# Own weights beside the turned rows in one bank, their turn behind the output products, values products with 128 columns

## The chip, the cores and the metric

The kernel runs on one core of a Trainium2 chip. The metric is the device time of one execution in microseconds (us). A core has TensorE (PE; its weight loads are shown apart as PEld), VectorE (DVE), ScalarE (ACT), GpSimd (POOL) and SyncE (SP, which issues DMAs). Products land in PSUM, which has eight banks; VectorE and ScalarE copy from there. TensorE's clock has two granted levels, 1.2 and 2.4 GHz, shown as 0.50 and 1.00.

## What is computed

An attention layer with a decaying state, and behind it two mixture-of-experts layers over the same 3072 tokens. The change lies in the attention:

```python
for t in range(S):                                   # B=4, H=8, S=768, D=48
    kt, vt, rt, wt = (k[:, :, t], v[:, :, t], r[:, :, t], w[:, :, t])
    cur = np.einsum('bhd,bhe->bhde', u[None] * kt, vt)
    y[:, :, t] = np.einsum('bhd,bhde->bhe', rt, state + cur)
    state = wt[:, :, :, None] * state + np.einsum('bhd,bhe->bhde', kt, vt)
...
x = y as 3072 rows of 384                            # then:
x = moe(x, one expert of 8 by argmax of x @ w_gate)
return moe2(x, two experts of 8, with noise)
```

## The kernel before

The sequence is cut into chunks of C = 128 tokens, which makes NU = 24 units (six chunks of four batch rows). A unit holds all eight heads, as four pairs (HP = 4, `pr`), the two heads of a pair at partitions 0 and 64 of the turned inputs. The unit's output is a sum of three parts: products of the tokens of the same chunk (scores, masked, times values), products with the state carried in from the chunk before, and each token's own product, which is weighted by `r u k` summed over the head ("own weights").

One loop (line 850) runs over i = 0 to 24 as a software pipeline: it works on units i + 2, i, i - 1 and i - 2 at once. The schedule is written out by hand: each engine runs its instructions in the order in which the loop body issues them, and waits where an operand or a bank is not ready. SP issues the loads (three of 224 KB and one of 192 KB per unit) and the store of the unit's 128 output rows; POOL masks the scores and scatters table entries.

In TensorE's order a loop has:

- `scores(i)` (L645), eight products into the banks `sp0` and `sp1`; ScalarE copies them to `at`, POOL masks `at`.
- `kv(i-1)`: eight products of keys and values (L670) into the first columns of bank `pp`, then four products of `ub` and `q` (L673), which give the own weights per head pair, into columns 256 to 383 of the same bank. ScalarE copies those to `oT` (L676).
- `keys(i)`: four transposes (L658) into bank `kp`, copied by ScalarE to `kk` (L660).
- `xt(i-2)`: three transposes (L742) of the output rows `x` of unit i - 2 into bank `xp`, copied by ScalarE to `xT` (L744) for the gates.
- `own(i-1)`: one product that turns `oT`, so that tokens lie on partitions (L682), into columns 400 to 407 of bank `pp`.
- `yout(i-1)`: from the second chunk on eight products with the carried state (L713), then eight of the masked scores and the values (L720), into the double bank `b45`. A head needs 48 columns; the products read 96 (the values of the next head come along and are not used), the last head 48.
- `logits(i-2)`: products with the gates (L192) in column groups, and for the last unit of a group their turn (L197).

A product of 32-bit floats is two instructions in the trace. In VectorE's order a loop has the carried state (`carry_on`, L701), the first scan of unit i + 2 (L615), the output rows `x` of unit i - 2 (`rows_out`, L732, which reads bank `b45` and `sv`), the rest of `prep(i+2)` (L618 to L630), in twelve loops a split of expert weights on VectorE or POOL (L165), then `s` (`kv_add(i-1)`, L697, which reads bank `pp`) and `sv` (`bonus(i-1)`, L688, which reads the turned own weights). Units form groups of four, later of two. Three loops behind a group's last unit VectorE chooses the experts (`choose`, L202 to L264), woven into the list above; a loop later it places the tokens (`place`, L282 to L302). The ranks between them are products into bank `kp` (`rank`, L273). In the first four units ScalarE forms `s`.

`filler` (L771) issues products of 512 columns that nobody reads, in the first two loops and ahead of them. Behind the loop `early` begins the first expert's products (L177 to L179) in the same banks.

Of the kernel before, what the change touches and what calls it, by code (L numbers as in the profile page):

```python
# [9 lines left out]
F32 = mybir.dt.float32  # L10
# [9 lines left out]
B, H, S, D = 4, 8, 768, 48  # L20
N, DM, E, F = B * S, H * D, 8, 1024
C = 128
NC = S // C
NU = NC * B
HP = H // 2
PP = 112
KD = DM // 128
# [39 lines left out]
def rwkv_moe_kernel(ctx, tc, r, k, v, w, rT, kT, wT, rkv, u, g1, a1, a2, g2, noise, b1, b2, out):  # L67
    nc = tc.nc
# [9 lines left out]
    ident = con.tile([128, 128], F32, name="ident")  # L78
# [43 lines left out]
    def banks(pool, **plan):  # L122

        turns = {n: itertools.cycle(b) for n, b in plan.items()}
        return lambda name: pool.tile([128, 512], F32, name="b" + next(turns[name]))
# [370 lines left out]
    with ExitStack() as c2:  # L496
        pa = c2.enter_context(tc.tile_pool(name="pa", bufs=1, space=PSUM))
        ac = c2.enter_context(tc.tile_pool(name="ac", bufs=1))
        wk = c2.enter_context(tc.tile_pool(name="wk", bufs=2))
# [3 lines left out]
        T = {}  # L503
        NS = HP * (C + 1)
        bank = banks(pa, sp0="0", sp1="1", kp="2", pp="3", xp="6", lp="7")

        def bank2():

            return pa.tile([128, 2, 512], F32, name="b45")
# [4 lines left out]
        def quads(t, n=128):  # L514
            return t[:, 0:HP * n].rearrange("p (a b) -> p a b", a=HP)
# [3 lines left out]
        for i in range(3):  # L519
            t = ac.tile([PP, NS + 1], F32, name=f"decay{i}")  # L520
# [23 lines left out]
        start = []  # L544
        for i in range(2):
            t = ac.tile([PP, HP, C + 1], F32, name=f"start{i}")
# [4 lines left out]
        ub = ac.tile([PP, HP, 32], F32, name="ub")  # L551
# [38 lines left out]
        def fills(i):  # L590
            if i == 1:
                nc.vector.memset(z, 0.0)
                nc.vector.memset(empty, 0)
                nc.vector.memset(empty[:, :, 0], N)
            if i in (2, 3):
                clear_table((tab1, tab2)[i - 2])
            if i == 4:
                nc.sync.dma_start(xrow[0:N, DM:XW], noise)
            if i == 5:
                nc.sync.dma_start(xrow[N:N + 1, 0:DM], z[0:1, :])  # L600
            if i == 6:
                nc.sync.dma_start(xrow[N:N + 1, DM:XW], z[0:1, 0:E])
            if i == 8:
                u0 = EARLY + 3
                b, n = u0 % B, NU - u0
                nc.sync.dma_start(rows(xrow, (b * S + (NC - 1) * C) * XW, [[XW, C], [S * XW, n], [1, DM]]),
                                  z[:, None, :].to_broadcast([C, n, DM]))
# [52 lines left out]
                nc.scalar.copy(t["kk"], kp[:, :, 0:PP])  # L660

        def kv(i):

            t = T[i]
            p = bank("pp")
            if i < NU - B:
                pp = t["pp"] = quads(p[:PP], D)
                for pr in range(HP):
                    for r0, r1, c0 in ((0, 64, 0), (64, PP, D)):
                        nc.tensor.matmul(pp[r0:r1, pr, :], t["kk"][:, pr, r0:r1],  # L670
                                         t["v"][:, pr * 96 + c0:pr * 96 + c0 + D], start=True, stop=True)
            for pr in range(HP):
                nc.tensor.matmul(p[32 * pr:32 * pr + 32, 256:256 + C], ub[:, pr, :], t["q"][:, pr, :],  # L673
                                 start=True, stop=True)
            t["oT"] = wk.tile([128, C], F32, name="oT", bufs=1)
            nc.scalar.copy(t["oT"], p[:, 256:256 + C])  # L676
            t["own"] = p[:C, 400:400 + H]

        def own(i):

            t = T[i]
            nc.tensor.matmul(t["own"], t["oT"], ident.rearrange("p (a b) -> p a b", a=HP)[:, :, 0:2],  # L682
                             start=True, stop=True)

# [5 lines left out]
        def kv_add(i):  # L690
            t = T[i]
            if i < NU - B:
                t["s0"] = wk.tile([PP, HP, D], F32, name="s0", bufs=4)
                if i < B:
                    nc.scalar.copy(t["s0"], t["pp"])
                else:
                    nc.vector.tensor_tensor(t["s0"], t["pp"], carry[i % B], OP.add)  # L697
# [5 lines left out]
        def yout(i):  # L703

            t = T[i]
            c, b = divmod(i, B)
            y = bank2()
            y = y.rearrange("p h (a d) -> p h a d", a=HP)
            if c:
                for pr in range(HP):  # L710
                    for hh in range(2):
                        r0 = 64 * hh
                        nc.tensor.matmul(y[:, hh, pr, 0:2 * D], t["R"][r0:r0 + D, pr, :],  # L713
                                         wide[b][r0:r0 + D, pr:pr + 2, :].rearrange("p a d -> p (a d)"),
                                         start=(pr == 0), stop=False, skip_group_check=True)
            for pr in range(HP):
                for hh in range(2):
                    h = 2 * pr + hh
                    n = min(2, H - h) * D
                    nc.tensor.matmul(y[:, hh, pr, 0:n], t["at"][:, hh, pr, :], t["v"][:, h * D:h * D + n],  # L720
                                     start=(c == 0 and pr == 0), stop=True, skip_group_check=True)
            t["y"] = y[:, :, :, 0:D]
# [12 lines left out]
            for g in T.get("eg", ()):  # L735
                tc.declare_no_dep(st.ins, g.ins, reason=APART)

        def xt(i):
            t = T[i]
            xp = quads(bank("xp"))[:, 0:KD]  # L740
            for k in range(KD):
                nc.tensor.transpose(xp[:, k, :], t["x"][:, k * 128:(k + 1) * 128], ident)  # L742
            t["xT"] = wk.tile([128, KD, C], F32, name="xT")
            nc.scalar.copy(t["xT"], xp)  # L744

        LAST, RT = {}, {}
        for u0, n in GROUPS:
# [102 lines left out]
        for i in range(NU + 1):  # L850
            on = [0 <= i - j < NU for j in range(4)]
            if i == 2:
                late_consts()
            fills(i)
            if i + 4 < NU:
                load(i + 4)
            if i + 3 < NU:
                load_rows(i + 3)
            rt = RT.get(i - 3)
            early_rt = rt if i == EARLY + 3 else None  # L860
            choose = rt.choose() if rt else none
            place = RT[i - 4].place() if i - 4 in RT and i != EARLY + 4 else none
            pre = prep(i + 2) if i + 2 < NU else none
            take(choose)
            if on[3]:
                carry_on(i - 3)
            take(choose)
            take(pre)
            if on[2]:
                rows_out(i - 2)  # L870
            for _ in range(3):
                take(choose)
                take(place, 3)
                take(pre)
            take(choose, 9)
            take(place, 9)
            take(pre, 9)
            if 8 <= i < 20:
                w_split(0, 0, *divmod(i - 8, 3), nc.gpsimd if i % 3 else nc.vector)
            if i in KICKS:  # L880
                kick()
            if on[0]:
                scores(i)
            if i == EARLY + EG:
                early_gather()
            if on[1]:
                kv(i - 1)
            if on[0]:
                keys(i)
            if on[2]:  # L890
                xt(i - 2)
            if rt:
                rt.exps()
            if on[1]:
                kv_add(i - 1)
                own(i - 1)
                yout(i - 1)
                bonus(i - 1)
            if on[2]:
                logits(i - 2)  # L900
            if rt:
                rt.rank(bank("kp"))
            if on[2]:
                turn(i - 2)
            if i - 4 in RT and i != EARLY + 4:
                waiting += [(RT[i - 4], j) for j in range(RT[i - 4].nj)]
            if early_rt:
                take(rt.place(), 9)
                waiting += [(rt, j) for j in range(rt.nj)]
            n = 2 if i < EARLY + 3 else len(waiting)  # L910
            for q, j in waiting[:n]:
                q.enter(j, "tab1")
            waiting = waiting[n:]
            if early_rt:
                early_load()
            if i < 2:
                filler(FB[i])
            if 5 <= i < 17 and (i - 5) % 3 == 0:
                w_load(0, 0, (i - 5) // 3)
            if i + 2 < NU:  # L920
                guard(i + 2)
# [5 lines left out]
        p = bank("kp")  # L927
# [166 lines left out]
    with ExitStack() as c2:  # L1094
        wk = c2.enter_context(tc.tile_pool(name="m1", bufs=2))
        bank = banks(psum, hp="01", tp="23", yp0="4", yp1="5", yp2="6", lp="7", up="01456")
# [185 lines left out]
    with ExitStack() as c2:  # L1282
        wk = c2.enter_context(tc.tile_pool(name="m2", bufs=1))
        bank = banks(psum, hp0="01", tp="23", hp1="45", yp="76")
# [163 lines left out]
```

## Time and profile before

| | us |
|---|---|
| median of 3 runs | 1031.95 |
| lowest and highest of them | 1031.88, 1053.61 |
| the profiled execution | 1035.67 |
| its span, first to last instruction | 1034.0 |

Over the span TensorE is busy for 970.8 us (94%), VectorE for 513.2, ScalarE for 396.5 and POOL for 404.8. The busy share mixes stages: the attention loop lies in the first 272 us, the expert layers behind it. A record of a matmul runs from its start to its modelled end, and pipelined records overlap, so the pace of a row of products is read from the distance of their starts.

### The profile page before, as it was taken

To read this page: it belongs to the slowest core of one execution; us is meant where nothing else is said; L and a number is where in the kernel's file an instruction comes from. 1 tells how busy PE (TensorE), PEld (TensorE's weight loads), DVE (VectorE), ACT (ScalarE), POOL (GpSimd) and SP (SyncE) were. 2 spreads that over 40 slices of the span, in tenths; PEclk is the share of its full clock that TensorE was granted. 3 is DMA by queue.
4 is the path that set the end of the run, shared out by engine and by line. 5 is a ranking of instruction groups with operands and counts; after the bars stand their busy time and mean duration, and the time that the engine had idled before them with its cause. 6 is when DMAs were issued, how large, how long until landed. Compare 5 with 4: busy or idle time off the path is not lost. (4 is left out here: it accounts for less than half of the span.)

```text
span 1034.0 us, 16583 instructions
## 1 busy us (share of the span) xinstructions
PE 970.8 (94%) x6212; PEld 867.7 (84%) x6212; DVE 513.2 (50%) x1162; ACT 396.5 (38%) x869; POOL 404.8 (39%) x562
## 2 busy tenths in 40 slices
PE   7789788988988999999999989999999999999996
PEld 4678677877778888999998778898989898989996
DVE  7955656465233456555666425715354453625220
ACT  4523433332213445455554315424343343434321
POOL 4214334223213165865885544233241514132303
PEclk8955665555559899999999989999999999999998
DMA  9717344330105555767564145453544434444303
GB/s 207 208 57 180 86 114 122 78 86 16 38 20 152 163 113 154 168 184 191 153 138 146 23 107 135 138 100 90 122 95 93 106 95 87 121 78 138 39 6 42
DMA packets 91100, 113.40 MB, mean 110 GB/s; under 512 B 26002, under 2 KB 68895, under 8 KB 91000
## 3 DMA queue, kind: packets, MB, share of 16 engines
q1 hardware_dynamic: 65848, 80.87, 28.1%
q0 software_dynamic: 25152, 31.27, 16.6%
q8 instruction: 54, 0.88, 0.4%
q14 instruction: 46, 0.38, 0.2%
HBM read 86.96 MB, written 25.78 MB: 109 GB/s over the span
## 5 line engine op out<-in xcount | busy, mean ns | idle before, releaser
L108 POOL DMA_INDIRECT out<-yo,ent x54 | 84.5, 1566 | 276.8 <-ACT yo L1339 224.5
L177 PE MATMUL b<-xhi,w1h 128*128 128x512 f32 (+8 forms) x384 | 133.1, 347 | 0.0
L179 PE MATMUL b<-xhi,w1l 128*128 128x512 f32 (+8 forms) x384 | 132.2, 344 | 0.0
L178 PE MATMUL b<-xlo,w1h 128*128 128x512 f32 (+8 forms) x384 | 132.2, 344 | 0.0
L1083 DVE TENSOR_TENSOR xlo<-b,xhi 128x512 fp32r<-128x512 f32 (+8 forms) x48 | 27.1, 570 | 157.2 <-ACT xhi L1082 157.2
L650 POOL TENSOR_SCALAR_AFFINE_SELECT at<-at 128x512 f32<-128x512 f32 x48 | 45.0, 958 | 132.2 <-ACT at L649 132.2
L1339 ACT ACTIVATE yo<-b,ent 128x384 f32<-128x384 f32 (+1 forms) x48 | 27.9, 581 | 167.6 <-issue 128.2
L1326 PE MATMUL b<-w2h,hah 128*128 128x384 f32 x256 | 89.2, 348 | 0.4 <-PEq L1274 0.4
L1328 PE MATMUL b<-w2h,hal 128*128 128x384 f32 x256 | 87.3, 341 | 0.0
L1327 PE MATMUL b<-w2l,hah 128*128 128x384 f32 x256 | 87.2, 341 | 0.0
L108 POOL DMA_INDIRECT tab<-en,si x60 | 77.8, 1296 | 19.1 <-issue 14.0
L177 PEld LDWEIGHTS b<-xhi,w1h 128*128 128x128 f32 x384 | 72.3, 188 | 11.8 <-issue 3.1
L178 PEld LDWEIGHTS b<-xlo,w1h 128*128 128x128 f32 x384 | 72.4, 189 | 8.8 <-DVE xlo L1083 0.2
L179 PEld LDWEIGHTS b<-xhi,w1l 128*128 128x128 f32 x384 | 72.3, 188 | 8.6
L177 PE MATMUL b<-hh,w2h 128*128 128x224 f32 (+7 forms) x216 | 75.4, 349 | 3.4 <-PEq L950 3.4
L177 PE MATMUL b<-xh,w1h 128*128 128x224 f32 (+7 forms) x216 | 77.2, 358 | 0.2 <-ACT xh L1129 0.2
L720 PE MATMUL b<-v,at 128*128 128x96 f32 (+1 forms) x384 | 77.3, 385 | 0.0
L720 PEld LDWEIGHTS b<-v,at 128*128 128x128 f32 x384 | 73.7, 295 | 3.2 <-issue 2.7
L178 PE MATMUL b<-xl,w1h 128*128 128x224 f32 (+7 forms) x216 | 74.3, 344 | 0.1
L179 PE MATMUL b<-xh,w1l 128*128 128x224 f32 (+7 forms) x216 | 74.2, 343 | 0.0
L178 PE MATMUL b<-hl,w2h 128*128 128x224 f32 (+7 forms) x216 | 73.2, 339 | 0.0
L179 PE MATMUL b<-hh,w2l 128*128 128x224 f32 (+7 forms) x216 | 73.1, 339 | 0.0
(221 smaller groups left out, 2246.4 us busy)
## 6 DMA issues: line engine op xcount, KB each, us to landing
raw<-in_a SPq DMA_DIRECT2D x32, 768.0 KB, 6.0
raw<-in_b SPq DMA_DIRECT2D x30, 768.0 KB, 5.0
decay<-in_wT SPq DMA_DIRECT2D x24, 224.0 KB, 4.5
kT<-in_kT SPq DMA_DIRECT2D x24, 224.0 KB, 4.4
rT<-in_rT SPq DMA_DIRECT2D x24, 224.0 KB, 4.3
v<-in_rkv SPq DMA_DIRECT2D x24, 192.0 KB, 4.4
xrow<-x SPq DMA_DIRECT2D x24, 192.0 KB, 4.3
out<-z SPq DMA_DIRECT2D x6, 768.0 KB, 10.1
```

Of the source, the lines that this page charges most:

```text
L108: st = nc.gpsimd.indirect_dma_start(out=table, out_offset=bass.IndirectOffsetOnAxis(ap=idx, axis=0), in_=src, in_offset=None, bounds_check ...
L177: nc.tensor.matmul(ps, st[0], mv[0], start=start, stop=False)
L178: nc.tensor.matmul(ps, st[0], mv[1], start=False, stop=False)
L179: nc.tensor.matmul(ps, st[1], mv[0], start=False, stop=stop)
L650: nc.gpsimd.affine_select(at[:, hh], at[:, hh], [[0, HP], [1, C]], OP.is_gt, 0.0, base=0, channel_multiplier=-1)
L720: nc.tensor.matmul(y[:, hh, pr, 0:n], t["at"][:, hh, pr, :], t["v"][:, h * D:h * D + n], start=(c == 0 and pr == 0), stop=True, skip_group ...
L1083: nc.vector.tensor_tensor(t["lo"][:, k], p[:, 0:n], t["hi"][:, k].bitcast(F32), OP.subtract)
L1326: nc.tensor.matmul(parts[0], h[:, f, sl], wh, start=(f == 0), stop=False)
L1327: nc.tensor.matmul(parts[0], h[:, f, sl], wl, start=False, stop=False)
L1328: nc.tensor.matmul(parts[0], l[:, f, sl], wh, start=False, stop=(f == NF - 1))
L1339: nc.scalar.activation(o, y, AF.Copy, scale=wgt2[:q, e, j:j + 1])
```

## The change

Four edits, which go together:

- The four products of `ub` and `q` (L673) leave bank `pp` and `kv`. They stand behind the transposes of `xt`, in the free fourth quarter of bank `xp`, and one ScalarE copy of up to 512 columns takes both to a tile of KD + 1 parts.
- `own` runs behind `yout`, and writes its eight columns to bank `kp`.
- The ranks of a group go to bank `xp`.
- The values products read 128 columns where the row of values has them (heads 0 to 5), 96 for head 6, 48 for head 7. The extra columns are not used.

```diff
         def kv(i):
             t = T[i]
-            p = bank("pp")
             if i < NU - B:
-                pp = t["pp"] = quads(p[:PP], D)
+                pp = t["pp"] = quads(bank("pp")[:PP], D)
...
-            for pr in range(HP):
-                nc.tensor.matmul(p[32 * pr:32 * pr + 32, 256:256 + C], ub[:, pr, :], t["q"][:, pr, :],
-                                 start=True, stop=True)
-            t["oT"] = wk.tile([128, C], F32, name="oT", bufs=1)
-            nc.scalar.copy(t["oT"], p[:, 256:256 + C])
-            t["own"] = p[:C, 400:400 + H]
 
         def own(i):
             t = T[i]
+            t["own"] = bank("kp")[:C, 0:H]
             nc.tensor.matmul(t["own"], t["oT"], ident.rearrange("p (a b) -> p a b", a=HP)[:, :, 0:2],
                              start=True, stop=True)
...
                     h = 2 * pr + hh
-                    n = min(2, H - h) * D
+                    n = min(128, DM - h * D)
                     nc.tensor.matmul(y[:, hh, pr, 0:n], t["at"][:, hh, pr, :], t["v"][:, h * D:h * D + n],
                                      start=(c == 0 and pr == 0), stop=True, skip_group_check=True)
...
-        def xt(i):
-            t = T[i]
-            xp = quads(bank("xp"))[:, 0:KD]
-            for k in range(KD):
-                nc.tensor.transpose(xp[:, k, :], t["x"][:, k * 128:(k + 1) * 128], ident)
-            t["xT"] = wk.tile([128, KD, C], F32, name="xT")
-            nc.scalar.copy(t["xT"], xp)
+        def xt(i, j=None):
+
+            xp = quads(bank("xp"))
+            n = KD
+            k0 = 0 if i is not None else KD
+            for k in range(k0, KD):
+                nc.tensor.transpose(xp[:, k, :], T[i]["x"][:, k * 128:(k + 1) * 128], ident)
+            if j is not None:
+                for pr in range(HP):
+                    nc.tensor.matmul(xp[32 * pr:32 * pr + 32, KD, :], ub[:, pr, :], T[j]["q"][:, pr, :],
+                                     start=True, stop=True)
+                n += 1
+            t = wk.tile([128, KD + 1, C], F32, name="xT")
+            nc.scalar.copy(t[:, k0:n], xp[:, k0:n])
+            if i is not None:
+                T[i]["xT"] = t[:, 0:KD]
+            if j is not None:
+                T[j]["oT"] = t[:, KD]
...
             if on[0]:
                 keys(i)
-            if on[2]:
-                xt(i - 2)
+            if on[1] or on[2]:
+                xt(i - 2 if on[2] else None, i - 1 if on[1] else None)
             if rt:
                 rt.exps()
             if on[1]:
                 kv_add(i - 1)
+                yout(i - 1)
                 own(i - 1)
-                yout(i - 1)
                 bonus(i - 1)
             if on[2]:
                 logits(i - 2)
             if rt:
-                rt.rank(bank("kp"))
+                rt.rank(bank("xp"))
```

## Rows read from the trace of the kernel before

**Rows 1.** The page: span, and granted TensorE clock in 40 equal slices, in tenths.

```profile
span 1034.0 us, 16583 instructions
...
PEclk8955665555559899999999989999999999999998
```

**Rows 2.** Windows by stage: stretch, its us, engines' busy us (instructions), clock, DMA, GB/s.

```profile
16.45:44.92 28.47, 24.84 (x285) 19.32 (x284) 28.06 (x44) 15.41 (x41) 10.35 (x36) 1.00 0.86 208
44.92:272.36 227.44, 199.58 (x1585) 170.87 (x1582) 126.43 (x270) 77.14 (x190) 70.73 (x88) 0.56 0.36 95
272.36:310.00 37.64, 32.37 (x202) 28.25 (x200) 12.28 (x64) 6.79 (x23) 7.97 (x17) 0.55 0.07 19
```

**Rows 3.** Windows of single loops; busy us in the order PE, PEld, DVE, ACT, POOL.

```profile
32.20:38.56 6.36, 5.47 (x74) 4.61 (x71) 6.33 (x10) 3.90 (x10) 1.79 (x2) 1.00 0.92 189
...
182.56:194.09 11.53, 11.53 (x90) 10.16 (x87) 5.98 (x11) 4.38 (x10) 4.84 (x7) 0.50 0.38 63
207.22:222.31 15.09, 12.21 (x96) 10.43 (x95) 10.34 (x22) 3.76 (x10) 1.54 (x3) 0.50 0.28 74
```

**Rows 4.** Waits, 44.92 to 272.36: us in total, times, longest us.

```profile
PE b L682 <- DVE s L697: 23.4, 10, 5.3
```

**Rows 5.** Timeline of TensorE: start, us, engine, line, tiles out<-in, shape, count.

```profile
12.75 3.78 PE L771 MATMUL b<-sind 112*128 112x512 f32 x4 [0.18 <-ACT at L649]
...
296.18 0.42 PE L178 MATMUL b<-xl,w1h 128*128 128x224 f32 x1
...
299.87 0.27 PE L179 MATMUL b<-xh,w1l 128*128 128x224 f32 x1
```

**Rows 6.** Windows again: a stretch in which TensorE stood idle.

```profile
110.00:114.60 4.60, 0.00 (x0) 0.00 (x0) 4.50 (x11) 0.45 (x3) 1.34 (x3) 0.72 0.67 186
```

**Rows 7.** Timeline of TensorE in a loop at 1.2 GHz.

```profile
186.98 0.85 PE L742 MATMUL b<-ident,x 128*128 128x128 f32 x3
...
189.94 3.65 PE L720 MATMUL b<-v,at 128*128 128x96 f32 x16
193.51 0.65 PE L192 MATMUL b<-xT,g1s 128*32 128x128 f32 x6
```

**Rows 8.** Timeline of TensorE and VectorE at 2.4 GHz.

```profile
139.69 1.14 PE L713 MATMUL b<-carry,R 48*128 48x96 f32 x16
139.80 0.56 DVE L688 TENSOR_TENSOR sv<-v,b 128x384 f32<-128x384 f32 x1 [0.85 <-PE b L682]
...
140.54 1.23 DVE L615 TENSOR_TENSOR_SCAN g<-decay,sind 112x516 f32<-112x516 f32 x1
...
140.76 1.99 PE L720 MATMUL b<-v,at 128*128 128x96 f32 x16
...
142.78 0.56 DVE L732 TENSOR_TENSOR x<-b,sv 128x384 f32<-128x384 f32 x1 [1.01 <-PE b L720]
143.02 1.16 PE L645 MATMUL b<-R,ke 48*128 48x128 f32 x16
...
144.71 0.42 PE L673 MATMUL b<-q,ub 112*32 112x128 f32 x8
...
145.50 0.49 PE L742 MATMUL b<-ident,x 128*128 128x128 f32 x3
...
147.96 0.39 PE L682 MATMUL b<-ident,oT 128*128 128x8 f32 x2 [1.96 <-DVE s L697]
```

**Rows 9.** Groups by line on VectorE, 44.92 to 272.36: count, busy us, mean ns.

```profile
L252 DVE SCALAR_TENSOR_TENSOR qo<-d,first 128x32 f32<-128x32 f32 (+1 forms) x6 | 3.3, 542 | 0.0
...
L246 DVE TENSOR_REDUCE mx<-L 128x4 f32<-128x32 f32 (+1 forms) x6 | 1.1, 175 | 0.0
L282 DVE TENSOR_TENSOR sl<-rk,base 128x32 f32<-128x32 f32 (+1 forms) x5 | 0.9, 189 | 8.2 <-ACT rk L277 8.2
...
L298 DVE CAST slot<-sf 128x4 int32<-128x4 f32 (+1 forms) x5 | 0.8, 158 | 0.0
```

## Prediction

> **What bounds the kernel now.** The page comes first. It gives the span, and its clock line shows the granted TensorE clock of 40 slices: behind the first two slices come ten of five and six tenths, close to 1.2 GHz, the lower of the two levels, and from slice 13 on eights and nines, close to 2.4 GHz [rows 1]. The low run is the attention loop. The windows by stage say it in numbers: in its first 28 us the loop runs at 1.00; from 44.92 to 272.36, the 18 loops i = 5 to 22, at 0.56 and with 227.44 us; the two expert layers behind it are not touched by the change [rows 2]. So the question is what 18 loops cost.
>
> Next, single loops. At the lower level the loop that starts at 182.56 takes 11.53 us with TensorE busy for all 11.53, while VectorE is busy for 5.98. At the higher level the loop that starts at 32.20 took 6.36 us, with VectorE busy for 6.33 (it has no carry products yet). A loop in which a group of tokens is routed, the one at 207.22, took 15.09, with TensorE busy for 12.21 [rows 3]. At the lower level TensorE is the bound, at the higher one VectorE nearly is.
>
> The waits say where the missing 2.9 us of the routed loop go: the turn of the own weights (L682) waits for VectorE's sum `s` (L697), 23.4 us over these loops [rows 4]. The two share no data. They share the bank `pp`, and L697 stands at the end of VectorE's list for the loop, behind the routing.
>
> What did TensorE do before its clock rose or fell? It rose at 16.45 behind fillers of 512 columns, and near 299.8 behind up-products of 224 columns, whose records go from 0.42 to 0.27 us [rows 5]. It fell around 112, in a stretch of 4.6 us in which TensorE had nothing to do and VectorE worked for 4.5 [rows 6]; after that it is half again for a loop or more. The values products (L720) of the loop at 182.56, 3.65 us without a pause, brought no rise [rows 7]. The Trainium skill ("TensorE: Matmul & The Clock Gate", Part 1) has the gate opened by TensorE's recent activity; the loop at 182.56, busy from end to end at 0.50, shows that what the profile counts as busy does not settle it.
>
> **The change, part by part.**
>
> *Values products with 128 columns.* Twelve of the 16 instructions of L720 in a loop go from 96 to 128 columns (heads 0 to 5; two instructions to a product). At the lower level they start 0.22 us apart (16 from 189.94 to 193.51). The transposes L742, which also load 128 columns of weights but move 128 columns, start 0.21 apart (0.85 us for three, the last with its tail) [rows 7]. So the pace is the weight load's, and 32 more columns fit under it. From below: nothing. From above: at the filler's 3.78 us / 4 / 512 = 1.85 ns a column [rows 5], 12 x 32 x 1.85 = 0.71 us a loop, 17 us in 24 loops. I take nothing, since L742 has the very form.
>
> The Trainium skill (same page, "Back-to-back issue gap") lets the gap between matmuls grow with their columns. By that rule the wider products would cost the upper bound, and the sum below would be 17 us worse where the clock stays low; the row of L742 speaks against it.
>
> What they may bring is the clock. After the change this stretch streams its columns without the holes that 96 columns leave under each weight load, as the fillers and the up-products did. No row shows this form at this place, so the effect is bounded from both sides: no rise at all (11.53 us a loop stays) or the higher level from the middle of each values stretch on. I take the second, because the two forms nearest to it were each followed by a rise.
>
> *The own weights' turn behind the output products, in the keys' bank.* The wait for L697 is gone from TensorE: L713 and L720 follow the transposes at once, and the 23.4 us [rows 4] become work under which VectorE finishes its list. In its new bank the turn waits for ScalarE's copy of the keys, done some microseconds earlier. What is late next is `bonus`: it now follows L720 instead of preceding it. On VectorE the carry, the first scan and the rows' sum `x` are queued behind it, and the next loop's transposes wait for `x`. So a loop has a chain from `x` to `x`. At the higher level [rows 8]: transposes 0.49, u-products 0.42, carry products 1.07 (139.69 to 140.76), values products 1.99, turn 0.39, together 4.36; then `sv` to the end of the scan 1.97 (139.80 to 140.54, and 1.23), `x` 0.56; about 0.2 for the hand-overs (estimate). Sum 7.1 us. TensorE's own work at this level is 2.48 (143.02 to 145.50) + 0.49 + 1.07 + 2.26 (140.76 to 143.02) + 0.39 = 6.7, and VectorE's 6.33 [rows 3] plus `s`, 0.35 (estimate, the carry's like), is 6.7. So the chain decides, at 7.1, by a little. At the lower level the chain is about 7.1 for TensorE's part (186.98 to 193.51 is 6.53 [rows 7], and 0.6 for the u-products) and 2.7 for VectorE's, 9.8, hidden under 11.53 of TensorE work.
>
> *u-products beside the turned rows, one copy.* The same four products, moved past the keys and behind the wait for `x`; ScalarE does one copy instead of two, some 0.2 us less of an engine that is busy for 4.4 us of 11.53 [rows 3]. No DMA is moved, so SP's and POOL's queues keep their order. Worth nothing by itself; its 0.42 is in the chain above. The ranks in the rows' bank: they wait for the copy of the turned rows, already asked for by the gates' products; nothing.
>
> **Sum.** Loops 5 to 22, at the higher level: 18 x 7.1 = 127.8. Six of them choose experts: eight lines of VectorE, 2.1 us together, the means from 0.54 to 0.18 [rows 9], and a wait for the gates' turn of between 0 and the 2.9 us by which TensorE idled in the routed loop; I take half, so 6 x 3.5 = 21.0. Five place tokens: nine lines, 1.5 us [rows 9], 7.5. In these eleven VectorE's list is longer than TensorE's, TensorE idles again, and the clock can fall; then the chain's TensorE part is 7.1 instead of 4.4 once, 2.7 us. From below 0, from above 11 x 2.7 = 30; I take 15, since VectorE's longer list covers part of it. Together 171.3 against 227.4: 56 us less. Behind the loops, from 272.36 to 310.00 at 0.55 [rows 2], two more pairs of carry and values products run, 5.5 us each at the lower level and 3.0 at the higher, so 0 to 5.1 us; I take 2. In all 58. The profiled execution took 1035.67 us, its span 1034.0; 1035.67 - 58 = 977.7. The median of the runs, 1031.95, is 3.7 lower, so the forecast is **974 us**. Its own range: the falls at 0 or 30, the choosing waits at 0 or 2.9 and the tail give -26 to +26, so 948 to 1000.
>
> **Rivals.**
>
> 1. *The clock rises in the values products and falls again in every loop*, because the chain leaves TensorE idle in front of `x`. Speaks for it: the fall around 112. Against: in the plain loop the idle time is 7.1 - 6.7 = 0.4 us, not 4.6. Then 18 x 2.7 = 48.6 instead of 15: saved 56 - 33.6 + 2 = 24, so 1008.
>
> 2. *The wider products do not raise the clock*; only the wait goes. TensorE stays the bound at 11.53 a loop, and 23.4 us come back: 1008.5. Speaks for it: 3.65 us of these products never brought a rise.
>
> 3. *The wait moves and nothing is gained*: `bonus` behind L720 makes VectorE late in the routed loops by what TensorE got back. Against: 9.8 against 11.53. About 1029.
>
> 4. *Slower*: the columns add to the weight load in L720. Price 17 us, so 1049; it decides once the clock stays low and less than 17 of the 23.4 us come back. Against: L742.
>
> **How the numbers follow.** Forecast 0.64, rival 1 0.14, rival 2 0.12, rival 3 0.06, rival 4 0.04. The time is the forecast's, 974. About 2% (20.6 us) is what a measurement of this kernel can tell from no change, so faster means under 1011.3: nearly all of the forecast, and some six tenths of rivals 1 and 2, which lie close to the bound: 0.79. Slower 0.04, the rest 0.17. The range leaves out rivals 3 and 4 and a tenth at the lower end of all cases: 950 to 1016.
>
> **What would show it.** Right: the granted clock between 45 and 270 mostly 1.00, the loop's records of L645 about 7 us apart, L720 of 128 columns still 0.21 to 0.22 us apart at the lower level, L682 no longer waiting for L697, VectorE's `sv` waiting for L682 instead. Wrong: a clock of 0.5 through the loops with L720 unbroken (rival 2); a fall in plain loops (rival 1); L720's starts at 0.26 us or more (rival 4). The most doubtful step is the clock's rise, which rests on the likeness of forms; next the eleven routed loops, whose idle time is summed and not read.

## The result and the profile after

The changed kernel took 966.04 us (median of four runs, 959.49 to 970.37); the kernel before, run beside it, 1038.4. The ratio is 0.9317, with a 95% interval of 0.9209 to 0.9426. Here and below a ratio and its interval are of the fast runs alone, a median is of all runs. The forecast was 974 with a range of 950 to 1016. So time and direction came out. The reasons came out only in part: the step that carried the sum credited the wider values products with the clock, and the runs below give most of the gain to the other half of the change.

The profiled execution took 959.49 us. The page, span and granted clock in 40 slices; the run of fives and sixes of [rows 1] is gone:

```profile
span 957.9 us, 16567 instructions
...
PEclk8999989988898999999999999999999999999998
```

The windows by stage, as in [rows 2] (stretch, its us, busy us and instructions of PE, PEld, DVE, ACT and POOL, clock, DMA share, GB/s). The first line is the loops i = 5 to 22 again. The second holds the end of the attention and the first 20 us of the expert layers, whose first up-product starts at 207.90, the third the rest of them:

```profile
41.86:191.31 149.45, 129.01 (x1585) 108.61 (x1582) 130.13 (x272) 74.29 (x173) 68.55 (x88) 0.94 0.54 146
191.31:228.00 36.69, 29.23 (x245) 26.52 (x243) 13.44 (x68) 7.07 (x23) 9.87 (x19) 0.81 0.14 34
228.00:957.90 729.90, 699.35 (x4078) 637.60 (x4076) 334.21 (x765) 288.65 (x599) 310.15 (x402) 0.98 0.47 112
```

The 18 loops take 149.45 us instead of 227.44, at a clock of 0.94 instead of 0.56. (When both kernels were profiled again on one chip, the loops took 152.22 and 218.07, so the 78 us of this pair were 66 there.) TensorE and VectorE are now busy for the same time, 129 and 130 us.

The waits in these loops (us in total, times, longest). The 23.4 us of [rows 4] have no successor on the turn (now L675), which waits for nothing; TensorE waits for `x` (L725) instead, and VectorE's `sv` (L681) for the turn:

```profile
PE b L737 <- DVE x L725: 15.1, 13, 3.5
...
DVE sv L681 <- PE b L675: 12.4, 6, 3.9
```

One loop at 2.4 GHz, from 50.00 to 57.18, as a timeline (start, us, engine, line, tiles; in brackets the idle time before it). In this loop a group chooses its experts:

```profile
50.00 1.16 PE L645 MATMUL b<-R,ke 48*128 48x128 f32 x16
...
50.81 1.22 DVE L615 TENSOR_TENSOR_SCAN g<-decay,sind 112x516 f32<-112x516 f32 x1
...
51.95 0.53 DVE L725 TENSOR_TENSOR x<-b,sv 128x384 f32<-128x384 f32 x1
...
52.54 0.55 PE L737 MATMUL b<-ident,x 128*128 128x128 f32 x3 [0.25 <-DVE x L725]
53.01 0.43 PE L740 MATMUL b<-q,ub 112*32 112x128 f32 x8
53.37 1.14 PE L706 MATMUL b<-carry,R 48*128 48x96 f32 x16
...
54.43 1.99 PE L713 MATMUL b<-v,at 128*128 128x128 f32 x16
...
56.26 0.35 PE L675 MATMUL b<-ident,xT 128*128 128x8 f32 x2
56.30 0.69 DVE L630 TENSOR_TENSOR R<-rT,cp 112x512 f32<-112x512 f32 x1
...
56.91 0.35 DVE L690 TENSOR_TENSOR s<-b,carry 112x192 f32<-112x192 f32 x1
...
57.18 0.54 DVE L681 TENSOR_TENSOR sv<-v,b 128x384 f32<-128x384 f32 x1
```

TensorE waits 0.25 us for `x` and no more. The values products (L713), 12 of the 16 with 128 columns, take 1.99 us, as with 96 columns in [rows 8]. The turn is over at 56.61, yet `sv` starts at 57.18: it stands behind R and `s` on VectorE, so in this loop VectorE's own list sets the pace.

At the lower level the 16 values products take 3.65 us, the figure of [rows 7]:

```profile
138.59 3.65 PE L713 MATMUL b<-v,at 128*128 128x128 f32 x16
```

### The profile page after: what moved, and what is told of

It reads as the page before. It is cut to its first block, busy times and chain, and to the rows that moved or that the text cites. A ratio compares the mean times of both kernels' runs of the same rounds, so it can differ in the third digit from the quotient of the medians.

```text
span 957.9 us, 16567 instructions
## 1 busy us (share of the span) xinstructions
PE 893.9 (93%) x6212; PEld 797.6 (83%) x6212; DVE 514.8 (54%) x1162; ACT 393.0 (41%) x846; POOL 404.2 (42%) x562
## 5 line engine op out<-in xcount | busy, mean ns | idle before, releaser
L108 POOL DMA_INDIRECT out<-yo,ent x54 | 84.6, 1566 | 276.6 <-ACT yo L1343 224.3
L108 POOL DMA_INDIRECT tab<-en,si x60 | 78.8, 1313 | 19.4 <-issue 14.6
L165 DVE TENSOR_TENSOR w1l<-raw,w1h 128x512 fp32r<-128x512 f32 x92 | 61.6, 684 | 23.9 <-ACT w1h L164 23.4
L1144 DVE SCALAR_TENSOR_TENSOR hl<-b,hh 128x224 fp32r<-128x224 f32 (+7 forms) x64 | 35.8, 559 | 69.0 <-ACT hh L1143 58.7
L1096 DVE SCALAR_TENSOR_TENSOR hal<-b,hah 128x512 fp32r<-128x512 f32 x64 | 44.1, 690 | 50.3 <-ACT hah L1095 46.5
```

The costliest lines, as they stand in the source:

```text
L108: st = nc.gpsimd.indirect_dma_start(out=table, out_offset=bass.IndirectOffsetOnAxis(ap=idx, axis=0), in_=src, in_offset=None, bounds_check ...
L165: eng.tensor_tensor(c, a, b.bitcast(F32), OP.subtract)
L1096: nc.vector.scalar_tensor_tensor(l, p[:, 0:n], 0.0, h.bitcast(F32), OP.max, OP.subtract)
L1144: nc.vector.scalar_tensor_tensor(l, p[:, c], 0.0, h.bitcast(F32), OP.max, OP.subtract)
```

## The experiments

"Loops" below means the loops i = 5 to 22 of the profiled execution, from the first L645 of one to the first L645 of loop 23. A clock of k in a stretch means that the lower level was granted in 2(1 - k) of it. A fall is a change from the higher level to the lower, a low stay the time until the next rise. These runs stood on three chips, on which the kernel before had medians of 1029.68, 1055.62 and 1047.0 us; only runs of one chip are set beside each other, or ratios to the kernel before.

### The two halves alone: columns, order, bank

The first kernel is the one before with the columns alone:

```diff
-                    n = min(2, H - h) * D
+                    n = min(128, DM - h * D)
```

> Only the values products go from 96 to 128 columns; order and banks are those before. Theory A (the wide products raise the clock, and that is most of the gain): the loops 5 to 22, 227 us before and 149 after the change, take 165 to 185 us with a mean clock of 0.8 or more, and the time is 975 to 1000 us; the wait of the turn for the sum s stays, some 15 to 25 us. Theory B (the order and the banks do it: TensorE no longer stands idle, so its clock holds): the clock stays near 0.56 and the time within 10 us of before. If the wider products cost time of their own, the time is over that of before by up to 17 us.

The second is the change with that line left as it was, so all that moves banks and order, and 96 columns.

> The change whole, but with the values products at 96 columns as before. Theory A: the clock stays near 0.5 to 0.6 in the loops, only the wait for the sum s is gone, 23 us, so 1005 to 1015 us. Theory B: nearly the whole gain, under 985 us, with a clock over 0.8.

The third is the kernel before with the turn in the keys' bank, at its old place ahead of the output products:

```diff
-            t["own"] = p[:C, 400:400 + H]
...
         def own(i):
             t = T[i]
+            t["own"] = bank("kp")[:C, 0:H]
```

> The kernel before with one edit: the own weights' turn writes to the keys' bank instead of the bank of the keys' and values' products, at its old place ahead of the output products; 96 columns. It measures the wait by itself. Theory A: the wait for the sum s, 23.4 us, goes, nothing else moves: 1005 to 1015 us. If the place of the turn mattered as well as its bank, less than half of it: over 1020 us. Theory B: if no idle TensorE is enough to hold the clock, under 985 us.

Measured on one chip (the kernel before 1029.68):

| kernel | median us | ratio, interval | loops us | clock there |
|---|---|---|---|---|
| columns alone | 1010.54 | 0.9837 (0.9766 to 0.9909) | 209.71 | 0.73 |
| bank of the turn alone | 989.88 | none given | 174.47 | 0.74 |
| order and banks, 96 columns | 978.48 | 0.9518 (0.9457 to 0.958) | 168.88 | 0.79 |

The columns alone are worth 19 us, the order and the banks 51, the turn's bank by itself 40 (36 to 52 by its four runs, 977.86 to 993.91). So most of the 51 us is the bank; the new place, the moved products and the single copy are not told apart by these runs. The columns alone met neither theory: they gain more than 10 us, but the loops stay far above 185. The order with 96 columns came out as theory B had it, under 985, and the bank alone between its two theories. The waits of the kernel with the columns alone show what was left undone there:

```profile
PE b L682 <- DVE s L697: 40.5, 16, 5.2
```

TensorE now stands before the turn 16 times, 10 in [rows 4], and for 40.5 us instead of 23.4. The faster TensorE gets there, the longer it waits for `s`, and its clock falls again: eleven falls in these loops, each followed by a rise. With the order and 96 columns it is the other way round: the windows of the kernel with 96 columns show 1.00 at first, then few falls, each with a long stay at the lower level:

```profile
46.61:75.60 28.99, 24.39 (x333) 20.26 (x330) 27.29 (x56) 14.62 (x34) 11.83 (x16) 1.00 0.73 215
75.60:85.80 10.20, 10.20 (x79) 8.98 (x79) 7.15 (x11) 3.83 (x9) 3.46 (x5) 0.50 0.78 192
102.90:113.20 10.30, 10.30 (x79) 9.07 (x81) 9.43 (x20) 3.86 (x9) 5.16 (x7) 0.50 0.89 241
147.30:171.20 23.90, 23.21 (x176) 20.35 (x170) 13.48 (x26) 8.53 (x19) 6.25 (x6) 0.50 0.28 77
188.20:215.49 27.29, 25.39 (x172) 21.55 (x169) 12.39 (x39) 7.33 (x19) 10.29 (x14) 0.50 0.10 29
```

On top of the order the columns are worth some 15 us more: with the splits moved as below, 971.72 without them and 956.2 with them on one chip, by ratios whose intervals do not touch.

In the first profile of the changed kernel the four low stays in the loops were 3.4 to 6.8 us long. The reading at this point was that the two halves do different things: taking away the wait for `s` takes away idle stretches behind which the clock falls, and the columns end the low stay sooner once it has fallen. The second half of it is looked at again below.

### The turn ahead of the output products

The changed kernel, with the turn in its new bank but at its old place:

```diff
-                yout(i - 1)
                 own(i - 1)
+                yout(i - 1)
```

> The change whole, but the turn of the own weights ahead of the output products, as before (in the keys' bank, so that it doesn't wait for s). My chain theory: the loop after the change is bound by the chain from x to x, 7.1 us, in which the turn stands behind the output products; with the turn ahead VectorE's product with the values runs under them, so the chain loses about 1.5 us and plain loops fall from 7.2 to the 6.7 us of TensorE's and VectorE's work: 5 to 10 us less than the change, 955 to 962. Rival: the turn waits for ScalarE's copy of the turned rows, some 0.8 us in which TensorE idles in every loop: the same or up to 10 us more.

It took 969.17 us, 0.9436 of the kernel before (0.9365 to 0.9507), its loops 166.56 at 0.86. No gain over the changed kernel's 0.9317, whose interval overlaps, so the theory that the turn's place costs 5 to 10 us in a chain from `x` to `x` missed. The row fits the rival: the turn then waits in each of the 18 loops for the copy of the turned rows.

```profile
PE b L675 <- ACT xT L744: 13.7, 18, 1.3
```

### Why the clock still falls: VectorE's lines beside GpSimd

Two of the four falls in the changed kernel's loops follow the same picture. Its timeline in loop 8:

```profile
65.33 3.65 DVE L615 TENSOR_TENSOR_SCAN g<-decay,sind 112x516 f32<-112x516 f32 x1
...
65.98 1.31 POOL L165 TENSOR_TENSOR w1l<-raw,w1h 128x512 fp32r<-128x512 f32 x1
...
67.20 2.20 POOL L650 TENSOR_SCALAR_AFFINE_SELECT at<-at 128x512 f32<-128x512 f32 x2
...
69.48 0.55 PE L737 MATMUL b<-ident,x 128*128 128x128 f32 x3 [3.14 <-DVE x L725]
```

VectorE's scan takes 3.65 us instead of the 1.22 of the loop above, while GpSimd runs a split of expert weights (L165) and then L650; `x` is late, TensorE is idle for 3.14 us, and the clock falls at about 70.7. In loop 16 the carry takes 2.31 us (0.35 else) and the scan 1.65. But a split beside the scan is not enough: in loop 10, and likewise in loop 11, one started during the scan and left it at its length:

```profile
84.06 1.22 DVE L615 TENSOR_TENSOR_SCAN g<-decay,sind 112x516 f32<-112x516 f32 x1
...
84.86 1.49 POOL L165 TENSOR_TENSOR w1l<-raw,w1h 128x512 fp32r<-128x512 f32 x1 [5.87 <-ACT w1h L164]
```

In the kernel before the 17 scans of these loops took 1.23 us on average: the change brought the scan and the split to the same time. To test whether the split does it, all splits in the loops go to VectorE:

```diff
-                w_split(0, 0, *divmod(i - 8, 3), nc.gpsimd if i % 3 else nc.vector)
+                w_split(0, 0, *divmod(i - 8, 3), nc.vector)
```

> The changed kernel with all splits of the expert weights in the loops on VectorE, where two of three ran on GpSimd. In the loops 8 and 16 of the changed kernel VectorE's scan (L615) took 3.65 and 1.65 us instead of 1.22, and its carry (L694) 2.31 instead of 0.35, while GpSimd ran a split (L165); behind both TensorE waited for x for over 3 us and its clock fell. Theory A, that the work of GpSimd stretches VectorE's lines: the long scans go away, the falls of loops 8 and 16 with them, and the loops 5 to 22 take 137 to 145 us although VectorE has some 8 splits of 0.7 us more; the time is 4 to 12 us lower. Theory B, that VectorE's own list is what makes TensorE late: the falls stay or grow, the loops take 151 to 158, the time is up to 8 us higher.

Beside it the changed kernel itself, and the carry products with 128 columns (a longer tile, the same place):

```diff
-        wide = [ac.tile([PP, HP + 1, D], F32, name=f"carry{b}") for b in range(B)]
+        wide = [ac.tile([PP, HP + 2, D], F32, name=f"carry{b}") for b in range(B)]
...
-                        nc.tensor.matmul(y[:, hh, pr, 0:2 * D], t["R"][r0:r0 + D, pr, :],
-                                          wide[b][r0:r0 + D, pr:pr + 2, :].rearrange("p a d -> p (a d)"),
+                        nc.tensor.matmul(y[:, hh, pr, 0:128], t["R"][r0:r0 + D, pr, :],
+                                          wide[b].rearrange("p a d -> p (a d)")[r0:r0 + D, pr * D:pr * D + 128],
```

> The changed kernel once more, nothing altered. In its first profiled execution the two expert layers took 750 us from the first up-product to the end, against 738 in the kernel before and 735 to 739 in four variants, so that 12 of the 88 us gained in front of them were given back. Theory A, chance of one execution (the start of a gather or of the weights' transfers): the expert layers take 735 to 742 us this time, the loops 5 to 22 take 145 to 155 again, and the span is 943 to 952. Theory B, a property of the changed kernel (its earlier arrival at the experts finds something not ready): 748 to 752 again, the span 955 to 960.

> The changed kernel with the carry products widened too, from 96 to 128 columns (their extra 32 columns land in columns of the bank that nobody reads; the carry's tile is one block longer). Theory A, that TensorE's clock comes back after a fall as soon as an unbroken run of 128-column products has passed: the carry products stand in front of the values products, so the clock comes back up to 2 us earlier after each of four falls and may skip a fall; the loops 5 to 22 take 141 to 149 us, the time is 0 to 8 us lower. Their own price is nothing, since at the lower level they are paced like the values products, whose 96 and 128 columns both took 3.65 us for 16. Theory B, that the carry products of 48 rows count little and their columns cost: no fall less, 16 of them take more than 1.14 us at the higher level, the time is the same or up to 3 us higher.

> The changed kernel with both: carry products of 128 columns and all splits on VectorE. Theory A of both: the loops 5 to 22 at 7.2 to 7.5 us each, 132 to 140 us, hardly a fall, the time 8 to 16 us lower than the changed kernel's. Theory B of both: 0 to 8 us higher.

Measured on one chip (the kernel before 1055.62):

| kernel | median us | ratio, interval | loops us | clock there |
|---|---|---|---|---|
| changed kernel | 986.54 | 0.9333 (0.9194 to 0.9471) | 161.61 | 0.85 |
| carry products 128 | 974.32 | 0.9273 (0.9181 to 0.9365) | 150.92 | 0.93 |
| splits on VectorE | 968.67 | 0.9256 (0.912 to 0.9392) | 142.88 | 0.94 |
| both | 971.51 | 0.9228 (0.9117 to 0.9339) | 142.76 | 0.95 |

The theory of the splits held: no scan or carry was stretched in these loops, and the falls of loops 8 and 16 went; one new fall came, in loop 15, which the next profile of this kernel did not have. The intervals of all four overlap, so the splits were run again, with the changed kernel, on a third chip:

> The changed kernel once more, the other half of the comparison of the expert layers, and the base for the kernel with the splits moved: loops 5 to 22 at 145 to 165 us; the expert layers within 4 us of the kernel before on this chip if their length belongs to the chip, 8 us or more longer if the earlier arrival costs.

> The changed kernel with all splits of the expert weights in the loops on VectorE, again, on one chip with the changed kernel: the loops 5 to 22 at 140 to 146 us, no scan over 1.3 us, no fall in loops 8 and 16, the time 4 to 18 us below the changed kernel's. If the gain on the earlier chip was that of a disturbed changed kernel, under 3 us here.

There the changed kernel took 964.75 us, 0.9232 of the kernel before (0.9175 to 0.9289), and the one with the splits on VectorE 956.2, 0.9115 (0.9062 to 0.9168). The intervals do not touch: this version beats both kernels, the changed one by 8.5 us in the medians. The groups of the scan and of the carry, first of the changed kernel (count, busy us, mean ns, idle before):

```profile
L615 DVE TENSOR_TENSOR_SCAN g<-decay,sind 112x516 f32<-112x516 f32 x17 | 23.7, 1392 | 0.0
L694 DVE TENSOR_TENSOR carry<-s,g 112x192 f32<-112x192 f32 x18 | 8.6, 479 | 0.0
```

and of the one with the splits on VectorE:

```profile
L615 DVE TENSOR_TENSOR_SCAN g<-decay,sind 112x516 f32<-112x516 f32 x17 | 20.8, 1224 | 0.0
L694 DVE TENSOR_TENSOR carry<-s,g 112x192 f32<-112x192 f32 x18 | 6.3, 349 | 0.0
```

All waits of the transposes (L737), in the same order, the changed kernel first:

```profile
PE b L737 <- DVE x L725: 15.1, 13, 3.5
...
PE b L737 <- ACT at L649: 1.1, 1, 1.1
PE b L737 <- DVE sl L282: 0.3, 1, 0.3
PE b L737 <- DVE d L249: 0.2, 1, 0.2
```

```profile
PE b L737 <- DVE x L725: 6.5, 9, 2.3
...
PE b L737 <- ACT at L649: 3.2, 3, 1.1
PE b L737 <- DVE d L249: 2.7, 3, 1.3
...
PE b L737 <- DVE sl L282: 0.3, 1, 0.3
```

With some 5 us less of stretched lines (2.9 and 2.3) the transposes wait 4.0 us less in all (12.7 instead of 16.7), though VectorE has eight more splits of 0.68 us. The loops are 9.6 us shorter (152.22 to 142.60), and by their clocks of 0.92 and 0.95 some 10 us less of them lies at the lower level. The windows of this version show what is left, one stretch at the full clock, up to a point in loop 20, and then the rest to the end of loop 22:

```profile
43.49:161.20 117.71, 105.19 (x1391) 87.97 (x1389) 112.84 (x239) 66.41 (x152) 44.14 (x64) 1.00 0.65 175
161.20:186.09 24.89, 21.85 (x196) 18.41 (x196) 14.63 (x42) 7.92 (x21) 12.55 (x17) 0.73 0.12 36
```

The wider carry products did not do what was hoped. They cost nothing visible (1.16 us for 16 at the higher level, 1.14 with 96 columns; 2.08 and 2.03 at the lower), but the falls of loops 8 and 16 stayed (one of the last loops had none), the loops are no shorter than the changed kernel's were in two other profiles (149.45 and 152.22), and with the splits moved they add nothing (142.88 and 142.76, where 132 to 140 was expected). That this kernel's 974.32 is below 986.54 is therefore not credited to them. The 161.61 us of the changed kernel on this chip have another cause: behind the same falls its low stays were 17 us from 72.2 on and 48 us from 184.8 on. So 128 columns do not always end a low stay soon.

### The splits moved, with 96 columns

The kernel with order and banks and 96 columns, with the splits on VectorE as well. It asks whether the columns are needed to hold the clock, or only behind a fall.

> The change without its 128 columns (values products of 96), and with all splits of the expert weights in the loops on VectorE. Theory A, that the columns are worth something only behind a fall, by bringing the clock back: with the falls of loops 8 and 16 gone the loops up to 14 run like those of the same kernel with 128 columns (7.2 to 8 us each, clock 1.00), the loops 5 to 22 take 145 to 160 us (168.9 without the move of the splits), the rest lying in the long low stays behind the last falls, and the time is 6 to 20 us below that of the order alone. Theory B, that the columns hold the clock up in every loop: falls in plain loops between 40 and 120, the loops take 165 us or more.

On the third chip it took 971.72 us, 0.9253 (0.9194 to 0.9312); its profiled execution was the longest of its four (981.37, the others 965.89 to 977.32), so its loops, 158.90 us at 0.81, are rather too long. Windows of it:

```profile
46.15:96.10 49.95, 45.38 (x610) 37.87 (x609) 47.23 (x99) 28.26 (x66) 16.11 (x25) 1.00 0.68 190
96.10:106.40 10.30, 10.30 (x81) 8.69 (x77) 9.57 (x21) 3.58 (x9) 5.33 (x6) 0.50 0.90 243
130.30:150.80 20.50, 20.50 (x154) 17.84 (x157) 15.67 (x25) 7.27 (x17) 10.15 (x11) 0.50 0.59 133
174.70:205.05 30.35, 28.46 (x195) 23.76 (x194) 14.33 (x43) 8.03 (x21) 12.44 (x17) 0.50 0.12 36
```

For 50 us, six loops of 6.9 to 8.5 us, 96 columns stand at 2.4 GHz without a fall: the columns are not what holds the clock there. But two falls came, at 96.1 and 130.3, that the same kernel with 128 columns did not have on this chip (1.00 up to 161.20), and the low stays are 10 to 58 us long, where that kernel had two of 6.8. The second of these falls lies in loop 15, in which the kernel with 128 columns had fallen once too, on the other chip. The theory was right for the plain loops and the long stays; that the columns also spare falls rests on the one at 96.1 and is not shown. Why the loop at 91.15 falls with 96 columns and not with 128 stays open.

### Are the 12 us behind the loops given back?

In the profile of the changed kernel the expert layers, from the first up-product to the end, took 750.0 us, in the one before 738.2. On the second chip the changed kernel took 760.5 there, outside both ranges that had been expected. The kernel before was profiled again beside the changed kernel on the third chip:

> The kernel before, nothing altered, beside the changed kernel on one chip, for the length of the two expert layers. If that length belongs to the chip, both have the same within 4 us here (738 and 750 in their first profiles, 760 for the changed kernel on another chip). If arriving 70 us earlier costs the changed kernel something there, it is 8 us or more shorter in this one.

The windows of the expert layers there, the kernel before first:

```profile
285.88:1029.80 743.92, 713.45 (x4176) 652.90 (x4176) 340.80 (x796) 291.81 (x610) 316.91 (x410) 0.98 0.45 111
```

```profile
210.54:953.90 743.36, 710.51 (x4176) 649.79 (x4176) 340.79 (x796) 290.67 (x610) 317.18 (x412) 0.98 0.45 111
```

Half a microsecond apart, although one arrives 75 us earlier. So the length there does not follow from arriving early. It goes mostly with the chip, or with the time of the runs: 734.6 to 738.9 in the four profiles of the first chip, 760.5 to 766.8 in the four of the second, 743.4 to 750.9 in the four of the third. Within one chip it moves by 4 to 7 us, and what moves it was not traced further. The 11.8 us between the first two profiles lie inside this spread.

## Why the prediction was right, and where it was not

Against the first pair of profiles, the spans 1034.0 and 957.9:

| step | taken | measured |
|---|---|---|
| 18 loops, with choosing and placing | 127.8 + 21.0 + 7.5 = 156.3 | 134.1 (18 x 7.45, the mean of the 14 loops without a fall) |
| falls of the clock | 15 | 15.3 (four loops of 45.1 us together, less 4 x 7.45) |
| loops 5 to 22 | 171.3, 56 less | 149.45, 78.0 less |
| up to the first up-product | 2 less | 6.9 less (23.46 to 16.59) |
| ahead of loop 5 | nothing | 3.1 less (44.92 to 41.86) |
| expert layers | nothing | 11.8 more (738.2 to 750.0) |
| together | 58 less | 76 less |

**Right by its own steps.** The wait of L682 is gone; TensorE waits 15.1 us for `x` instead. The wider products cost nothing at either level: 1.99 and 3.65 us for 16, before and after, so the row of the transposes in [rows 7] was the right one to go by. The rule of the Trainium skill ("TensorE: Matmul & The Clock Gate", "Back-to-back issue gap") that the gap grows with the columns does not agree with these fp32 rows; rival 4, which had that price, is out. `sv` does wait for the turn, 12.4 us in six loops.

**The step that failed: what raises the clock.** This is the step that the prediction itself called the most doubtful. It let the 128 columns raise the clock, because the forms nearest to them had been followed by a rise, and let the removed wait give back its 23.4 us and no more. Measured alone, the columns are worth 19 us and the order and banks 51. The prediction had looked at the clock as something that a piece of work brings up. It also has to be kept up: each wait for `s` was an idle stretch behind which it could fall, as around 112 in [rows 6], and the wait had to be priced with the low loops that followed it. A loop at the lower level takes 11.53 us [rows 3], at the higher some 7.5: each loop spent low costs 4 us more. Rival 2 failed for the same reason. Its premise was that without the rise TensorE stays at 11.53 a loop, for 1008.5; the kernel without the columns took 978.48 and ran six loops at 2.4 GHz when the splits were out of the way. That the time came out is luck as far as this step goes: both halves were in the change, and the sum did not depend on which of them did the work. Part of the nearness of 974 and 966 is chance as well: in the first pair the loops gave 22 us more than was forecast, and the expert layers, put at nothing, took 11.8 back.

**A mis-sized term: the choosing and placing loops.** With the plain part of the loops they were given 156.3 us and took 134.1. The loop at 50.00, with its 7.18 us, does not confirm the plain loop's 7.1, since it chooses. The distance from one `x` to the next tells more, since VectorE's lines of one loop lie between them. Here are four in a row of the kernel with the splits on VectorE, all at 2.4 GHz:

```profile
98.75 0.53 DVE L725 TENSOR_TENSOR x<-b,sv 128x384 f32<-128x384 f32 x1
...
105.47 0.53 DVE L725 TENSOR_TENSOR x<-b,sv 128x384 f32<-128x384 f32 x1
...
113.59 0.53 DVE L725 TENSOR_TENSOR x<-b,sv 128x384 f32<-128x384 f32 x1
...
121.49 0.53 DVE L725 TENSOR_TENSOR x<-b,sv 128x384 f32<-128x384 f32 x1
...
129.49 0.53 DVE L725 TENSOR_TENSOR x<-b,sv 128x384 f32<-128x384 f32 x1
```

All four have a split on VectorE. The first distance is a plain loop, 6.72 us; the second, 8.12, holds VectorE's wait for the gates' turn and the first lines of the choosing; the third, 7.90, the rest of the choosing; the fourth, 8.00, the placing. So a group costs 3.9 us over four plain loops here, where the prediction had 3.5 + 1.5. In the changed kernel the one plain loop without a fall, from the `x` at 101.30, takes 7.08 us, with a carry of 0.70: the 7.1 came out there, but not by the chain. In all these distances but the second VectorE stands still for some 0.1 us at most, so its list sets the pace. The rest of the 22 us lies mostly in the last loops (loop 22 took 5.90 us), where TensorE has no products of keys and values any more.

**Right in sum, half right in cause: the falls.** Fifteen microseconds were taken and 15.3 came, but not from eleven routed loops whose lists are too long. There were four falls. Two come from VectorE's lines stretched beside GpSimd: the test took the splits away from GpSimd, and with them both falls. The one in loop 21 has the prediction's cause. TensorE, without products of keys and values there, waited for `x` while VectorE worked through the lines of a choosing and a placing without a pause:

```profile
178.63 0.52 PE L737 MATMUL b<-ident,x 128*128 128x128 f32 x3 [2.48 <-DVE x L725]
```

The fall in loop 19 is not explained. With the splits moved two falls were left on the third chip, in the loops 20 and 21.

**Not foreseen.** The chain from `x` to `x` was to decide by a little, with the turn late for `sv`. In the loop at 50.00 VectorE's own list decides: the turn is over 0.57 us before `sv` starts. And the expert layers moved by 12 us between the first two profiles, which no view of one profile could have told; on one chip they were equal.

## What to carry to other kernels

A wait that leaves TensorE idle can cost more than its own length where the clock falls behind it (here 23.4 us of waiting, some 40 us of time), so price it with the slow work that follows, and look for it first in a bank that two unrelated tiles share. When a step brings two edits that aim at the clock, ask of each whether it keeps the clock from falling or brings it back, and try each alone. After a change that shifts the loop, look at single long instances of a line (the longest beside the mean), since two engines that had missed each other may now meet.

## What the runs showed of the hardware

- VectorE's scan of 516 columns with two inputs took 3.65 us instead of 1.22 in loop 8, when GpSimd's tensor-tensor started 0.65 us into it and its select followed, and the 192-column carry 2.31 instead of 0.35 in loop 16, with the tensor-tensor 0.21 us behind its start. In the loops 10 and 11 the tensor-tensor started 0.80 and 0.70 us into the scan; the scan kept 1.22 and 1.23 us, and the tensor-tensor took 1.49 and 1.58 instead of 1.31. With the tensor-tensor gone from GpSimd, the select still ran beside the scan and no scan was longer than 1.3 us in these loops. The Trainium skill ("SBUF — State Buffer", "Who interferes with whom") has VectorE instructions with two inputs in SBUF contend with GpSimd instructions that read it, and the one that starts later wait for the other. Loops 10 and 11 agree. In loops 8 and 16 the one that had started first became long; there GpSimd's scatter of table entries (L108) was still running when it started, spans on GpSimd are rough, and why it became long stays open.
- In fp32, 16 values products take the same time with 96 columns and with 128 in 12 of them, at both levels of the clock (1.99 and 3.65 us), and 16 carry products of 48 rows 1.14 and 1.16 us at the higher, 2.03 and 2.08 at the lower.
- With the same order of work the low stays after a fall were 10 to 55 us long with 96 columns and 3.4 to 6.8 with 128 in the first profile of the changed kernel. In its other two profiles they were 3.4 to 10.3 and 3.5 to 48 us, so this is a tendency in a few executions and no rule.
